# Three of four first mixings in three fp32r passes, POOL rounding and DVE subtracting, with a reordered first tile

## The chip, the cores and the metric

The kernel runs on one core of one Trainium2 chip. The metric is the device time of one execution in microseconds (us). Before the change it is 952.89 us, the median of three runs (951.13 to 954.56).

## The reference

Talking-heads attention, and behind it two feed-forward matmuls. Everything is fp32: q, k, v are 4 x 12 x 448 x 64, the two mixing matrices 12 x 12, `w_in` 768 x 2048 and `w_out` 2048 x 768. Cut to what matters:

```python
scores = np.matmul(q, k.transpose(0, 1, 3, 2)) / np.sqrt(64)
scores = np.einsum('bhij,hg->bgij', scores, w_pre)       # first mixing, over the heads
attn = np.exp(scores - scores.max(-1, keepdims=True))
attn = attn / (attn.sum(-1, keepdims=True) + 1e-09)
attn = np.einsum('bhij,hg->bgij', attn, w_post)          # second mixing
x = np.matmul(attn, v).transpose(0, 2, 1, 3).reshape(1792, 768)
h = x @ w_in
out = np.where(h >= 1, h, np.where(h <= -1, 0, (h + 1) ** 2 / 4)) @ w_out
```

The weights of the feed-forward part arrive as 64-bit floats and are turned into fp32 on the chip.

## The kernel before

**Tiles, blocks, groups.** The 448 query rows of each of the 4 batches are cut into tiles of 120, 120, 120 and 88 rows, 16 tiles in all. A tile is cut into blocks of up to 10 query rows with all 12 heads, so that a block fills 120 partitions (10 rows x 12 heads) with 448 keys. A tile of 120 rows has 12 blocks, one of 88 rows has 9; they are worked in three groups a tile, so there are 36 groups of four blocks and 12 of three, 48 groups and 180 blocks.

**One pass of the loop over groups** (`for n in range(NG + 2)`, L586) puts the work of several groups into each engine's queue in an order written out by hand. The scores of a tile lie in SBUF (`ssb`). `load_s` (L175) moves a block from there into the block layout by a DMA (queue SP). `pre` (L191) is the first mixing on TensorE (PE): `wpre` times the block. `row_max` (L202, VectorE, DVE) and `exps` (L207, ScalarE, ACT) make the softmax, `norm` (L213) the reciprocal sums on DVE and, on GpSimd (POOL), the second mixing's matrix scaled by them (`wr`, L221). `post` (L224) is the second mixing on PE and is run for the group before, behind `pre` of the present group. Then come the transposes and scores of later tiles, `pv` (the product with v) of earlier ones, and pieces of the conversion of `w_in` and of some of `w_out` (`convs`).

**The first mixing in two forms.** A block whose fp32 values go to PE as they are costs one fp32 matmul, which the trace shows as two records of L200. A block that `split` (L182) has cut into a high part (rounded to fp32r) and a low part (the difference) costs three fp32r matmuls (L198). `split` runs for group n + 1 while group n is worked, both of its operations on DVE: the cast at L187, the subtraction at L188. It takes the second and fourth block of a group (`[1::2]`; in a group of three the second alone), and group 0 has none: 82 blocks of 180. The four loads of a group are issued in the order 1, 3, 0, 2 (0, 2 for the missing ones in a group of three): first those that are split.

**The first tile.** The loads of q and k, ten matmuls of an identity matrix (`warm`, which computes nothing that is used), transposes of q and k with two warm matmuls ahead of each k pair but the first, scores of tile 0, loads of group 0, transposes of q of tile 1, 16 warm matmuls, and then the loop.

**The feed-forward part** goes in batches of 512, 512, 512 and 256 rows and 16 steps each; a step is `ffn1` (L419), `gate` (L431 to L436, ACT and DVE in turn, six dependent operations with the split), `ffn2` (L456) of the step before. In the first batch's steps the rest of `w_out` is converted: `lowest` (ACT, L288) writes a buffer `wk`, two of them, which the integer addition on POOL (L301) two steps later releases.

Of the kernel before, what the change touches and what calls it, by code (L numbers as in the profile page):

```python
# [9 lines left out]
F32 = mybir.dt.float32  # L10
F32R = mybir.dt.float32r
I32 = mybir.dt.int32
# [10 lines left out]
def tile_talking_heads_moe(  # L23
# [151 lines left out]
    def load_s(m):  # L175
        t, o, ni, c = blocks[m]
        n, nb = tiles[t][2:]
        x = ap_.tile([KM, S], F32, tag="s10", name="s10", bufs=8)
        nc.sync.dma_start(out=x[:ni * H], in_=ssb[t][o:n:nb])
        s10[m] = x  # L180

    def split(m):  # L182
        k = blocks[m][2] * H
        x = s10.pop(m)
        hi = ap_.tile([KM, S], F32R, tag="sh", name="sh", bufs=2)
        lo = ap_.tile([KM, S], F32R, tag="sl", name="sl", bufs=2)
        nc.vector.tensor_copy(out=hi[:k], in_=x[:k])  # L187
        nc.vector.tensor_tensor(out=lo[:k], in0=x[:k], in1=hi[:k].bitcast(F32), op=ALU.subtract)  # L188
        s10[m] = (hi, lo)

# [75 lines left out]
    def convert(st, p):  # L266

        def halves():
            w = st["raw"].bitcast(I32).rearrange("p (n t) -> p n t", t=2)
            return w[:, :, 0], w[:, :, 1]

        def scaled():
            lo, hi = halves()
            if "t" not in st:  # L280
                st["t"] = p.tile([128, CW], I32, tag="wt", name="wt", bufs=3)
            nc.scalar.activation(out=st["t"].bitcast(F32), in_=hi.bitcast(F32), func=AF.Copy,
                                 scale=2.0 ** -111)

        def lowest():
            lo, hi = halves()
            st["k"] = p.tile([128, CW], I32, tag="wk", name="wk", bufs=2)
            nc.scalar.activation(out=st["k"], in_=lo.bitcast(U32), func=AF.Copy, scale=2.0 ** -29)  # L288

        def shifted():  # L290
            nc.vector.tensor_single_scalar(out=st["t"], in_=st["t"], scalar=3,
                                           op=ALU.logical_shift_left)

        def sign():
            lo, hi = halves()
            t = st["t"]
            nc.vector.scalar_tensor_tensor(out=t, in0=hi, scalar=-0x80000000, in1=t,
                                           op0=ALU.bitwise_and, op1=ALU.bitwise_or)

        def add():  # L300
            nc.gpsimd.tensor_tensor(out=st["t"], in0=st["t"], in1=st.pop("k"), op=ALU.add)  # L301

        return [scaled, lowest, shifted, sign, add]
# [120 lines left out]
    def gate(s, ps):  # L424
        n = bat[steps[s][0]][1]
        a = pool['fw'].tile([128, TB], F32, tag="a", name="a")
        mx = pool['fw'].tile([128, TB], F32, tag="mx", name="mx")
        gh = pool['fw'].tile([128, TB], F32R, tag="gh", name="gh")
        gl = pool['fw'].tile([128, TB], F32R, tag="gl", name="gl")

        nc.scalar.activation(out=a[:, :n], in_=ps[:, :n], func=AF.Relu, scale=0.5, bias=c05)  # L431
        nc.vector.tensor_tensor(out=mx[:, :n], in0=ps[:, :n], in1=a[:, :n], op=ALU.max)  # L432
        nc.vector.scalar_tensor_tensor(out=mx[:, :n], in0=a[:, :n], scalar=1.0, in1=mx[:, :n],  # L433
                                       op0=ALU.min, op1=ALU.mult)
        nc.scalar.activation(out=gh[:, :n], in_=mx[:, :n], func=AF.Copy)  # L435
        nc.vector.tensor_tensor(out=gl[:, :n], in0=mx[:, :n], in1=gh[:, :n].bitcast(F32),  # L436
                                op=ALU.subtract)
        gs[s] = (gh, gl)
# [36 lines left out]
    with tc.manual_schedule():  # L475
# [22 lines left out]
                                base=H - 1, pattern=[[H, IB]], channel_multiplier=-1)  # L498

        def warm(n):  # L500
            ps = ps_q.tile([128, 128], F32, tag="q", name="ps_w")
            for m in range(n):
                nc.tensor.matmul(out=ps, lhsT=ident, rhs=ident, start=True, stop=True)

        warm(10)
        trans_q(0, 0)
        trans_k(0, 0)
        trans_q(0, 1)
        for hp in range(1, HP):
            warm(2)  # L510
            trans_k(0, hp)
        for g in range(3):
            scores(0, [2 * g, 2 * g + 1])()
# [16 lines left out]
        load_q(2)  # L530
        trans_q(1, 0)
        trans_q(1, 1)
        warm(16)
        at = {}
        late = {}

# [5 lines left out]
        for g in range(3):  # L542
            put(1, lambda g=g: load_v(0, g))
        for t in range(1, len(tiles)):
            for g in range(3):
                vis.setdefault(max(0, 3 * t - 4 + g), []).append((t, [2 * g, 2 * g + 1]))
            nb = tiles[t][0]
            if t >= 2:
                for g in range(2):
                    at.setdefault(3 * t - 6 + g, []).append(lambda t=t, g=g: trans_q(t, g))  # L550
                    if t + 1 < len(tiles):
                        put(3 * t - 6 + g, lambda t=t, g=g: load_q(t + 1, (g,)))
                if tiles[t][1] == 0:
                    for hp in range(HP):
                        put(3 * t - 7 + hp // 2, lambda nb=nb, hp=hp: load_k(nb, hp))
                        at.setdefault(3 * t - 6 + hp // 2, []).insert(0, lambda nb=nb, hp=hp: trans_k(nb, hp))
# [29 lines left out]
        for n in range(NG + 2):  # L586
            if n == NE:
                s_qk.close()
                pool['fp'] = ctx.enter_context(tc.tile_pool(name="ffn", bufs=2, side="right",
                                                            reuse_waits="tile"))  # L590
                pool['ps_h'] = ctx.enter_context(tc.tile_pool(
                    name="ps_h", bufs=2, space=PSUM, side="right", reuse_waits="tile"))
            if n == NG - 1:
                s_ss.close()
                pool['fw'] = ctx.enter_context(tc.tile_pool(name="ffw", bufs=2, side="right",
                                                            reuse_waits="tile"))
            share = nconv / (NE - 1)
            ms = groups[n] if n < NG else ()
            old = list(groups[n - 1]) if 0 < n <= NG else []
            if n + 1 < NG:  # L600
                for m in (*groups[n + 1][1::2], *groups[n + 1][::2]):
                    load_s(m)
            if ms:
                sm = ap_.tile([KM, 4], F32, tag="sm", name="sm", bufs=3)
            for m in ms:
                pre(m)
            nxt = list(groups[n + 1][1::2]) if n + 1 < NG else []
            for m in ms:
                row_max(m)
            if nxt:  # L610
                split(nxt.pop(0))
            for j, m in enumerate(ms):
                if j == 3:
                    post(old.pop(0)) if old else None
                exps(m, j, sm)
            if ms:
                norm(ms, sm)
            for m in nxt:
                split(m)
            convs(share * (n + 0.4))  # L620
            for m in old:
                post(m)
            for f in at.pop(n, ()):
                f()
            for t, g in vis2.pop(n, ()):
                pv(t, g)
            for f in [scores(t, hps) for t, hps in vis.pop(n, ())]:
                f()
            for f in late.pop(n, ()):
                f()  # L630
            convs(share * (n + 1))
            if n == NG:
                h = ffn1(0)
# [18 lines left out]
        for s in range(NS + 1):  # L652
            if s < NS:
                j, f = steps[s]
                if s > 0:
                    h = ffn1(s)
                    if f == NF - 1 and j + 1 < len(bat):
                        for kk in range(2, KDM):
                            split_x(j + 1, kk)
                            if kk == 2:  # L660
                                load_x(j + 1, KDM - 1)
                    gate(s, h)
                if j + 1 < len(bat):
                    if NF - 10 <= f < NF - 7:
                        load_x(j + 1, f - (NF - 10))
                    if NF - 6 <= f < NF - 4:
                        load_x(j + 1, f - (NF - 10) - 1)
            if s >= 1:
                ffn2(s - 1)
            if s + 2 < NS:  # L670
                split_w(s + 2)
            if s + NWE + 1 < NF:
                load_w(s + NWE + 1)
            for x in sorted(cv.pop(s, ()), key=lambda x: x[:3]):
                x[3]()
            if s < NS and j + 1 < len(bat):
                if NF - 8 <= f < NF - 6:
                    split_x(j + 1, f - (NF - 8))
# [29 lines left out]
```

## Time and profile before

| | |
|---|---|
| median of three runs | 952.89 us (951.13 to 954.56) |
| the profiled execution | 952.53 us |
| its span, first to last instruction | 950.6 us |
| PE busy | 932.6 us, 98% |
| DVE busy | 606.9 us, 64% |
| ACT busy | 543.0 us, 57% |
| POOL busy | 179.5 us, 19% |

The profiled execution is 1.93 us longer than its span, and 0.36 us below the median. Busy shares are means over the span: the attention part lasts until about 477 us and uses all engines and the DMA queues, the feed-forward part behind it uses PE nearly alone.

### The profile page before, as it was taken

Reading aid. Unit: us, or ns where it says so; the run is one execution under the profiler, and the core shown is the slowest. Engines: PE = TensorE matmul, PEld = TensorE weight load, DVE = VectorE, ACT = ScalarE, POOL = GpSimd, SP = SyncE. Lnnn points to the kernel's source line nnn. Section 1 sums busy time; section 2 is a strip of 40 time slices with the busy share of each in tenths; the row PEclk is TensorE's granted clock in tenths of the full one; section 3 lists DMA queues with packets and bytes.
Section 4 is the critical chain, followed back from the end, with each engine's and each line's share of the span. In section 5 each row is a group of like instructions: output and inputs, shape, how many; then the busy total and the mean of one; then the engine's idle time right before and its main releaser. Section 6 shows DMA issues by size and latency. Waiting matters only on the chain.

```text
span 950.6 us, 17979 instructions
## 1 busy us (share of the span) xinstructions
PE 932.6 (98%) x6754; PEld 785.2 (83%) x6754; DVE 606.9 (64%) x1113; ACT 543.0 (57%) x1146; POOL 179.5 (19%) x253
## 2 busy tenths in 40 slices
PE   7999999999999999999999989999999999999997
PEld 6677888888888888888888878888888888888997
DVE  3677867877778867765555566654455554445774
ACT  4576777776786767776655453533334433334553
POOL 0233234332434234331201212000000000000000
PEclk8999999999999999999999999999999999999999
DMA  5875766876677756745453440120000200000100
GB/s 90 223 220 165 202 188 205 244 208 180 202 214 229 209 159 205 235 159 147 140 205 140 157 164 1 38 74 1 12 12 12 83 1 1 12 1 20 54 1 34
DMA packets 118361, 115.21 MB, mean 121 GB/s; under 512 B 61700, under 2 KB 107268, under 8 KB 118276
## 3 DMA queue, kind: packets, MB, share of 16 engines
q1 hardware_dynamic: 115492, 113.38, 39.8%
q10 hardware_dynamic: 2784, 0.69, 0.5%
q8 instruction: 54, 0.88, 0.4%
q14 instruction: 31, 0.25, 0.1%
HBM read 55.85 MB, written 19.66 MB: 79 GB/s over the span
## 4 chain that ended last, share of the span: by engine, by line
PE 92%; DVE 2%; ACT 2%; DMA 1%; issue 1%; POOL 1%; SPq 0%; POOLq 0%; ACTq 0%
PE o L456 22%; PE ps_h L419 22%; PE ps_a L231 16%; PE ps_l L200 8%; PE ps_x L247 8%; PE ps_s L155 7%; PE ps_l L198 5%; PE ps_k L121 1%; DMA k<-in_k_dram 1%; PE ps_t L138 1%; POOL wo L301 1%; DMA s<-ssb 0%; DVE mx L433 0%; DVE wil L389 0%; DVE mx L432 0%
## 5 line engine op out<-in xcount | busy, mean ns | idle before, releaser
L221 POOL TENSOR_SCALAR wr<-wpost,rs 120x120 f32<-120x120 f32 x180 | 113.4, 647 | 306.7 <-DVE rs L217 273.2
L231 PEld LDWEIGHTS ps_a<-wr,e 120*112 120x112 f32 x1440 | 154.3, 177 | 6.7 <-issue 4.9
L231 PE MATMUL ps_a<-wr,e 120*112 120x120 f32 (+1 forms) x1440 | 155.2, 266 | 0.0
L210 ACT ACTIVATE e<-ps_l,nm 120x448 f32<-120x448 f32 x180 | 112.8, 632 | 56.8 <-DVE nm L204 56.2
L419 PE MATMUL ps_h<-xh,wil 128*128 128x512 f32 (+1 forms) x384 | 139.5, 363 | 0.0
L419 PE MATMUL ps_h<-xl,wih 128*128 128x512 f32 (+1 forms) x384 | 139.2, 362 | 0.0
L419 PE MATMUL ps_h<-xh,wih 128*128 128x512 f32 (+1 forms) x384 | 139.2, 362 | 0.0
L456 PE MATMUL o<-woh,gl 128*128 128x512 f32 x448 | 115.7, 339 | 4.4 <-DVE gl L436 4.4
L432 DVE TENSOR_TENSOR mx<-ps_h,a 128x512 f32<-128x512 f32 (+1 forms) x64 | 39.9, 624 | 119.3 <-ACT a L431 119.3
L456 PE MATMUL o<-woh,gh 128*128 128x512 f32 x448 | 115.5, 339 | 0.0
L456 PE MATMUL o<-wol,gh 128*128 128x512 f32 x448 | 115.3, 339 | 0.0
L204 DVE TENSOR_REDUCE nm<-ps_l 120x1 f32<-120x448 f32 x180 | 104.2, 618 | 14.7 <-PE ps_l L200 11.8
L431 ACT ACTIVATE a<-ps_h,c 128x512 f32<-128x512 f32 (+1 forms) x64 | 40.4, 632 | 112.7 <-PE ps_h L419 112.5
L233 ACT ACTIVATE aT<-ps_a 112x480 f32<-112x480 f32 x180 | 96.2, 591 | 3.0 <-PE ps_a L231 2.6
L200 PE MATMUL ps_l<-s,wpre 120*120 120x448 f32 x196 | 94.6, 567 | 1.6 <-ACT wk L288 1.6
L435 ACT ACTIVATE gh<-mx 128x512 fp32r<-128x512 f32 (+1 forms) x64 | 37.0, 578 | 92.8 <-DVE mx L433 92.8
L456 PEld LDWEIGHTS o<-woh,gl 128*128 128x128 f32 x448 | 75.1, 189 | 17.9 <-DVE gl L436 6.8
L456 PEld LDWEIGHTS o<-woh,gh 128*128 128x128 f32 x448 | 76.4, 188 | 9.8
L456 PEld LDWEIGHTS o<-wol,gh 128*128 128x128 f32 x448 | 76.3, 188 | 9.9
L247 PE MATMUL ps_x<-aT,v 112*64 112x120 f32 (+1 forms) x1536 | 83.8, 262 | 0.0
L419 PEld LDWEIGHTS ps_h<-xl,wih 128*128 128x128 f32 x384 | 72.4, 189 | 12.2
L419 PEld LDWEIGHTS ps_h<-xh,wih 128*128 128x128 f32 x384 | 72.4, 189 | 11.5
(75 smaller groups left out, 1462.7 us busy)
## 6 DMA issues: line engine op xcount, KB each, us to landing
s<-ssb SPq DMA_DIRECT2D x172, 210.0 KB
wraw<-in_moe_w_in_dram SPq DMA_DIRECT2D x32, 384.0 KB
raw<-in_moe_w_out_dram SPq DMA_DIRECT2D x20, 384.0 KB
wid<-wt SPq DMA_DIRECT2D x32, 192.0 KB
wi<-wid SPq DMA_DIRECT2D x16, 384.0 KB
v<-in_v_dram SPq DMA_DIRECT2D x12, 448.0 KB
out_dram<-osb SPq DMA_DIRECT2D x14, 384.0 KB
wraw<-in_moe_w_out_dram SPq DMA_DIRECT2D x12, 384.0 KB
```

The costliest lines, as they stand in the source:

```text
L155: nc.tensor.matmul(out=ps[s][:n], lhsT=qt[t][x][r, hp, :n], rhs=kt[b, hp][y][r, :], start=(m == 0), stop=(m == 2))
L198: nc.tensor.matmul(out=lps[m], lhsT=w[:k], rhs=y[:k], start=(j == 0), stop=(j == 2))
L200: nc.tensor.matmul(out=lps[m], lhsT=wpre[:k], rhs=x[:k], start=True, stop=True)
L204: nc.vector.tensor_reduce(out=nm, in_=lps[m], axis=AX.X, op=ALU.max, negate=True)
L210: nc.scalar.activation(out=e, in_=ps, func=AF.Exp, bias=nm, accum_out=sm[:, j:j + 1])
L221: nc.gpsimd.tensor_scalar_mul(out=w[:, :, :ni], in0=wpost[:, :, :ni], scalar1=rs[:, j:j + 1])
L231: nc.tensor.matmul(out=ps[:, r, :ni * H], lhsT=e[:, r * KP:(r + 1) * KP], rhs=w[:, :, :ni], start=True, stop=True)
L233: nc.scalar.activation(out=aT[t][:, :, :, c:c + ni], in_=ps[:, :, :ni * H].rearrange("q r (h i) -> q r h i", h=H), func=AF.Copy)
L247: nc.tensor.matmul(out=ps[s * D:(s + 1) * D, m, :n], lhsT=vt[b, g][:, 2 * m + s, r * D:(r + 1) * D], rhs=a[:, r, 4 * g + 2 * m + s, :n], s ...
L419: nc.tensor.matmul(out=ps[:, :n], lhsT=w[:, kk, :], rhs=x[:, :n], start=(c == 0), stop=(c == last))
L431: nc.scalar.activation(out=a[:, :n], in_=ps[:, :n], func=AF.Relu, scale=0.5, bias=c05)
L456: nc.tensor.matmul(out=o[bank][:, c0:c0 + ne], lhsT=g[:, t * 128:(t + 1) * 128], rhs=w[:, e0:e0 + ne], start=(f == 0 and m == 0 and c0 == ...
```

## The change

- `split` becomes two functions. The cast goes to POOL (`nc.gpsimd.tensor_copy`), the subtraction (`split_lo`) stays on DVE. Three blocks of four (two of three) are split: 129 blocks of 180. `sh` and `sl` get three buffers each instead of two, `s10`, the loaded blocks, six instead of eight.
- The loads of a group go in the order 1, 2, 3, 0.
- In the loop all casts of group n + 1 are queued on POOL ahead of the `wr` of group n.
- First tile: 12 warm matmuls at the start, three behind the first k pair, four and one ahead of the next two k pairs, none ahead of the others. The first third of tile 1's scores is computed ahead of the loop, where there were 16 warm matmuls; six stay.
- `wk` has six buffers in the feed-forward part.
- The last `ffn1` and its gate come one step earlier, ahead of `ffn2` of the third step from the end; its `gh` and `gl` get buffers of their own.

```diff
@@ load_s, split
-        x = ap_.tile([KM, S], F32, tag="s10", name="s10", bufs=8)
+        x = ap_.tile([KM, S], F32, tag="s10", name="s10", bufs=6)
...
-        hi = ap_.tile([KM, S], F32R, tag="sh", name="sh", bufs=2)
-        lo = ap_.tile([KM, S], F32R, tag="sl", name="sl", bufs=2)
-        nc.vector.tensor_copy(out=hi[:k], in_=x[:k])
+        hi = ap_.tile([KM, S], F32R, tag="sh", name="sh", bufs=3)
+        lo = ap_.tile([KM, S], F32R, tag="sl", name="sl", bufs=3)
+        nc.gpsimd.tensor_copy(out=hi[:k], in_=x[:k])
+        s10[m] = (x, hi, lo)
+
+    def split_lo(m):
+        k = blocks[m][2] * H
+        x, hi, lo = s10[m]
         nc.vector.tensor_tensor(out=lo[:k], in0=x[:k], in1=hi[:k].bitcast(F32), op=ALU.subtract)
         s10[m] = (hi, lo)
@@ lowest
-            st["k"] = p.tile([128, CW], I32, tag="wk", name="wk", bufs=2)
+            st["k"] = p.tile([128, CW], I32, tag="wk", name="wk", bufs=6 if p is pool.get("wp") else 2)
@@ gate
+        p, w, z = (pool['wp'], n, "z") if s == len(steps) - 1 else (pool['fw'], TB, "")
+        gh = p.tile([128, w], F32R, tag="gh" + z, name="gh" + z)
+        gl = p.tile([128, w], F32R, tag="gl" + z, name="gl" + z)
@@ the first tile
-        warm(10)
+        warm(12)
         trans_q(0, 0)
         trans_k(0, 0)
+        warm(3)
         trans_q(0, 1)
         for hp in range(1, HP):
-            warm(2)
+            warm((4, 1, 0, 0, 0)[hp - 1])
             trans_k(0, hp)
...
-        warm(16)
+        scores(1, [0, 1])()
+        warm(6)
...
-            for g in range(3):
+            for g in range(t == 1, 3):
                 vis.setdefault(max(0, 3 * t - 4 + g), []).append((t, [2 * g, 2 * g + 1]))
@@ the loop over groups
-                for m in (*groups[n + 1][1::2], *groups[n + 1][::2]):
+                for m in (*groups[n + 1][1:], groups[n + 1][0]):
                     load_s(m)
...
-            nxt = list(groups[n + 1][1::2]) if n + 1 < NG else []
+            nxt = list(groups[n + 1][1:]) if n + 1 < NG else []
             for m in ms:
                 row_max(m)
+            for m in nxt:
+                split(m)
             if nxt:
-                split(nxt.pop(0))
+                split_lo(nxt.pop(0))
...
                 norm(ms, sm)
             for m in nxt:
-                split(m)
+                split_lo(m)
@@ the feed-forward steps
-                if s > 0:
+                if 0 < s < NS - 1:
                     h = ffn1(s)
...
                     gate(s, h)
+
+                    if s == NS - 2:
+                        gate(NS - 1, ffn1(NS - 1))
```

The first place is PE's queue at the program's start, the difference of the two kernels. `ps_w` are the warm matmuls, `ps_t` the transposes of q, `ps_k` those of k.

```order
-L503 MATMUL ps_w<-ident 128x128 x10
+L512 MATMUL ps_w<-ident 128x128 x12
 L138 MATMUL ps_t<-ident,qraw 128x120 x3
 L121 MATMUL ps_k<-ident,k_86 128x112 x4
+L512 MATMUL ps_w<-ident 128x128 x3
 L138 MATMUL ps_t<-ident,qraw 128x120 x3
-L503 MATMUL ps_w<-ident 128x128 x2
+L512 MATMUL ps_w<-ident 128x128 x4
 L121 MATMUL ps_k<-ident,k_86 128x112 x4
-L503 MATMUL ps_w<-ident 128x128 x2
```

More warm matmuls stand ahead of the second k pair; the pairs behind the third follow each other with none between, where two stood ahead of each.

The second place is DVE's queue in the loop pass of group 2, in the kernel before. `nm` is the row maximum, `s_556` and `s_558` are two loaded blocks of group 3, `rs` the reciprocal sums, `wt` a weight chunk under conversion.

```order
L204 TENSOR_REDUCE nm<-ps_l 120x1 x4
L187 CAST sh<-s_556 120x448
L188 TENSOR_TENSOR sl<-s_556,sh 120x448
L216 TENSOR_SCALAR rs<-sm 120x4
L217 RECIPROCAL rs<-rs 120x4
L187 CAST sh<-s_558 120x448
L188 TENSOR_TENSOR sl<-s_558,sh 120x448
L291 TENSOR_SCALAR wt<-wt 128x384
L297 SCALAR_TENSOR_TENSOR wt<-wraw,wt 128x384
```

The same place in the changed kernel, where the three blocks of group 3 are `s_554`, `s_556` and `s_558`:

```order
L209 TENSOR_REDUCE nm<-ps_l 120x1 x4
L193 TENSOR_TENSOR sl<-s_554,sh 120x448
L221 TENSOR_SCALAR rs<-sm 120x4
L222 RECIPROCAL rs<-rs 120x4
L193 TENSOR_TENSOR sl<-s_556,sh 120x448
L193 TENSOR_TENSOR sl<-s_558,sh 120x448
L296 TENSOR_SCALAR wt<-wt 128x384
L302 SCALAR_TENSOR_TENSOR wt<-wraw,wt 128x384
```

The casts are gone from DVE and a third subtraction has come, behind the reciprocal sums like the second.

The third place is POOL's queue in the same stretch of the changed kernel, from the `wr` of group 1 to the casts for group 4. Before, POOL had only the rows of `wr` (four a group) and `wt` (the integer addition of a weight chunk) here, in this order.

```order
L226 TENSOR_SCALAR wr<-wpost,rs 120x120 x4
L306 TENSOR_TENSOR wt<-wt,wk 128x384
L187 CAST sh<-s_554 120x448
L187 CAST sh<-s_556 120x448
L187 CAST sh<-s_558 120x448
L226 TENSOR_SCALAR wr<-wpost,rs 120x120 x4
L306 TENSOR_TENSOR wt<-wt,wk 128x384
L187 CAST sh<-s_671 120x448
```

The three casts for group 3 now stand ahead of the `wr` of group 2 and of the addition behind it, and wait for group 3's loads.

## Rows read from the trace of the kernel before

**Rows 1.** The page: span, and busy time of each engine.

```profile
span 950.6 us, 17979 instructions
PE 932.6 (98%) x6754; PEld 785.2 (83%) x6754; DVE 606.9 (64%) x1113; ACT 543.0 (57%) x1146; POOL 179.5 (19%) x253
```

**Rows 2.** Busy time in stretches: length, engines, TensorE's granted clock, DMA share, GB/s.

```profile
35.00:40.00 5.00, 4.84 (x18) 3.02 (x19) 2.72 (x6) 2.63 (x6) 0.71 (x2) 0.66 0.92 242
40.00:50.00 10.00, 10.00 (x73) 8.27 (x72) 8.77 (x18) 8.59 (x22) 3.74 (x5) 1.00 0.97 209
...
200.00:300.00 100.00, 100.00 (x940) 82.38 (x939) 77.75 (x165) 73.53 (x183) 37.41 (x53) 1.00 0.69 203
```

**Rows 3.** Waits of PE: us in total, times, longest.

```profile
PE o L456 <- DVE gl L436: 4.4, 6, 1.2
PE ps_l L200 <- ACT wk L288: 1.6, 1, 1.6
```

**Rows 4.** The chain that ended last, 20 to 60 us: start, us, what.

```profile
55.34 0.98 PE ps_l L200 x2
56.33 0.61 PE ps_l L198 x3
56.94 0.75 PE ps_l L200 x2
```

**Rows 5.** Timeline of the first tile's end: start, us, engine, line, count.

```profile
21.56 1.24 DVE L164 COPY ssb<-ps_s 120x448 f32<-120x448 f32 x2 [0.35 <-PE ps_s L155]
...
22.88 3.28 SPq L179 DMA_DIRECT2D s<-ssb  x4
...
24.13 3.84 PE L503 MATMUL ps_w<-ident 128*128 128x128 f32 x32 [1.23 <-DVE ql L141]
...
27.80 3.17 PE L200 MATMUL ps_l<-s,wpre 120*120 120x448 f32 x8
```

**Rows 6.** Groups of instructions by line: the split on DVE.

```profile
L188 DVE TENSOR_TENSOR sl<-s,sh 120x448 fp32r<-120x448 f32 (+1 forms) x82 | 54.2, 661 | 2.8
...
L187 DVE CAST sh<-s 120x448 fp32r<-120x448 f32 (+1 forms) x82 | 31.0, 378 | 36.5 <-DMA s<-ssb 36.5
```

**Rows 7.** Groups of instructions on POOL, shapes apart.

```profile
L221 POOL TENSOR_SCALAR wr<-wpost,rs 120x120 f32<-120x120 f32 x172 | 107.8, 643 | 306.7 <-DVE rs L217 273.2 <-PE ps_a L231 19.5 <-PE ps_x L247 7.6
L301 POOL TENSOR_TENSOR wt<-wt,wk 128x384 int32<-128x384 int32 x44 | 44.2, 1007 | 0.0
...
masks.py:199 POOL TENSOR_SCALAR_AFFINE_SELECT ident<-ident 128x128 f32<-128x128 f32 x1 | 0.3, 294 | 0.1
...
L497 POOL TENSOR_SCALAR_AFFINE_SELECT mask<-mask 120x10 f32<-120x10 f32 x1 | 0.2, 196 | 0.1
```

**Rows 8.** Timelines of DVE and PE where a group's loads are late.

```profile
52.62 0.39 DVE L187 CAST sh<-s 120x448 fp32r<-120x448 f32 x1 [2.89 <-DMA s<-ssb]
...
171.28 0.39 DVE L187 CAST sh<-s 120x448 fp32r<-120x448 f32 x1 [1.95 <-DMA s<-ssb]
...
174.89 1.01 PE L200 MATMUL ps_l<-s,wpre 120*120 120x448 f32 x2
...
450.21 0.39 DVE L187 CAST sh<-s 120x448 fp32r<-120x448 f32 x1 [3.01 <-DMA s<-ssb]
...
451.62 0.98 PE L200 MATMUL ps_l<-s,wpre 120*120 120x448 f32 x2
```

**Rows 9.** Timeline, 196 to 216 us: POOL's `wr` and the `post` that reads it.

```profile
199.81 2.41 POOL L221 TENSOR_SCALAR wr<-wpost,rs 120x120 f32<-120x120 f32 x4 [5.33 <-DVE rs L217]
...
207.21 3.44 PE L231 MATMUL ps_a<-wr,e 120*112 120x120 f32 x32
```

**Rows 10.** Timeline of ACT in a feed-forward step.

```profile
563.20 0.55 ACT L288 ACTIVATE wk<-raw 128x384 int32<-128x384 uint32 x1 [2.61 <-POOL wo L301]
```

**Rows 11.** Timeline of the last steps: DVE's last `wil`, PE's last `ffn2`.

```profile
935.33 0.96 DVE L389 SCALAR_TENSOR_TENSOR wil<-wi,wih 128x768 fp32r<-128x768 f32 x1 [0.31 <-ACT wih L388]
...
943.64 0.61 PE L456 MATMUL o<-woh,gl 128*128 128x512 f32 x2 [0.40 <-DVE gl L436]
```

More of the change, by code (lines that the diff above doesn't have):

```diff
@@ L427, in gate @@
         mx = pool['fw'].tile([128, TB], F32, tag="mx", name="mx")
-        gh = pool['fw'].tile([128, TB], F32R, tag="gh", name="gh")
-        gl = pool['fw'].tile([128, TB], F32R, tag="gl", name="gl")
+        p, w, z = (pool['wp'], n, "z") if s == len(steps) - 1 else (pool['fw'], TB, "")
+        gh = p.tile([128, w], F32R, tag="gh" + z, name="gh" + z)
+        gl = p.tile([128, w], F32R, tag="gl" + z, name="gl" + z)
         nc.scalar.activation(out=a[:, :n], in_=ps[:, :n], func=AF.Relu, scale=0.5, bias=c05)
@@ L500, in warm @@
         def warm(n):
+            if n == 0:
+                return
             ps = ps_q.tile([128, 128], F32, tag="q", name="ps_w")
```

## The prediction

> **What bounds the kernel now.** The page comes first: PE is busy 932.6 of 950.6 us [rows 1]. Busy is no proof of a bound, so the stretches come next: from 200 to 300 us PE has no idle time at all, DVE is at 78%, ACT at 74%, POOL at 37% and the DMA engines at 0.69 [rows 2]. PE sets the pace of the attention part, with DVE as the nearest follower. PE's own waits say where it stands still later: 4.4 us for `gl` in the feed-forward part and 1.6 us once near 55 us [rows 3]. The rest of the loss lies ahead of 28 us and in one place behind: from 35 to 40 us the granted clock is 0.66 [rows 2], that is, PE ran about 3.4 of those 5 us at its lower level of 1.2 GHz. So the change can win in three ways: less PE work in the attention part, those 4.4 us, and the first tile.
>
> **First mixing, PE.** In the chain a split block takes 0.61 us (three passes), an unsplit one 0.75 us; the first block of a group, 0.98 us, stays unsplit [rows 4]. Of the 35 groups of four behind group 0, and of the 12 groups of three, each gets one more split block: 47 blocks, 0.14 us each. PE is the bound there, so this is taken in full, but for the three blocks of groups 1 to 3, which lie ahead of a load that PE waits for anyway (below): 44 x 0.14 = **6.2 us**. Bounds: 0, if the split arrives late, and 47 x 0.14 = 6.6.
>
> **The split, DVE.** 82 casts of 378 ns go (31.0 us) and 47 subtractions of 661 ns come (31.1 us) [rows 6]. DVE's total is unchanged, and as it had 22% idle [rows 2] I cost it at nothing. If that cover were gone, each further 0.1 us a group would cost 4.7 us in all.
>
> **The split, POOL.** 129 casts of 120x448 come; the trace has no such operation on POOL. Two simple selections without a second input took 196 ns for 10 elements a partition and 294 ns for 128 [rows 7], a slope of 0.83 ns, so 0.56 us for 448: the lower bound. The two-input integer addition took 1.007 us for 384 elements, which gives 1.17 us; `wr` took 643 ns for 120, which by its rate would be 2.4 us, the upper bound [rows 7]. The cast is one-input and streams like the selections; I take **0.7 us**. A group of four then asks 2.1 us for casts, 2.4 for `wr` [rows 9] and 1.0 for the addition, 5.5 us. The period is 9.2 us: `pre` of groups 16 and 46 start at 174.89 and 451.62 [rows 8], 30 groups apart. POOL has room.
>
> The casts stand ahead of `wr`, so what `wr` loses counts. Four `wr` began at 199.81 and the first is read at 207.21 [rows 9]: 7.4 us of slack for a delay of 2.1 us, or 3.5 at 1.17. No cost. DVE now waits for POOL ahead of its first subtraction, which delays the reciprocal sums by 0.7 - 0.38 = 0.3 us where the load is late: covered by the same slack. The third subtraction has most to lose. In the late group of 171.28 us the first load landed then; the last split block is wanted at 174.89 + 0.98 + 2 x 0.61 = 177.1 [rows 4, 8], 5.8 us on. Three casts and one subtraction in a row are 2.8 us (4.2 at 1.17). Hidden.
>
> The Trainium skill (GPSIMD Engine Reference, section 4.1) sends elementwise work to VectorE, and its key points say that POOL shares its SBUF interfaces with VectorE and contends with instructions of two SBUF inputs, which the subtraction is. No row here shows a POOL cast; by that rule, an estimate, every cast could stand behind a subtraction, 0.7 + 0.66 us, and a group would ask 7.5 us of POOL. That is still under the period, so the sum would be the same, and only the rival below comes nearer.
>
> **The loads' order.** Block 0, first in `pre`, now comes fourth instead of third (third instead of second in a group of three). SP issues the four loads in 3.28 us, 0.82 apart [rows 5]; as they land I put them 0.8 to 1.4 us apart. From 171.28 the fourth lands at 173.7 to 175.5, and PE wants it at 174.89 less 0.14: a toss-up, in the few groups that are this late. I take 0.3 us for all, 0 to 4 as bounds. In group 46 the first of three loads came at 450.21, after a wait of 3.01 us, and `pre` began at 451.62 [rows 8]: the second load had landed by then, the third by 453.0 at 1.4 apart. I take **-1.3 us** (0 to -1.6). Six buffers instead of eight cost nothing: the load that is fourth in the next group needs the buffer of a block whose subtraction lies a whole group back.
>
> **The first tile.** Tile 0's last scores leave DVE at 22.80 us, the first loads are issued at 22.88, and `pre` starts only at 27.80, behind 16 warm matmuls of 3.84 us [rows 5]. 32 records in 3.84 us are 0.24 us a matmul at full clock. Between the second k pair and the scores seven fewer stand: 1.7 us at full clock, 3.4 at half. Copies of k on ACT and DVE follow in their own time, so I let the loads start **1.5 us** earlier (1 to 2.2). Then the DMA queues take over: their share is 0.92 from 35 to 40 us and 0.97 from 40 to 50 [rows 2]. So the scores moved ahead and the shorter warm-up do not shorten the way to group 3, whose first load arrives at 52.62 after a wait of 2.89 us [rows 8], and for which PE waits 1.6 us [rows 3]. There I keep the 1.5 us, less 0.8 for the fourth load. PE idles longer in front of group 3 than before; if the clock falls there, half of some 3.4 us [rows 2], 1.7 us, goes. First tile: **+0.7 us**, bounds -1.0 and +3.3 (1.5 + 1.8 if the queues have room).
>
> **`wk`.** In each step of the first batch ACT stood 2.61 us at `lowest` until POOL's addition released a buffer [rows 10], and everything of ACT behind it, the gate among them, came late; five of PE's six waits for `gl` are these, 4.4 less the last of 0.40: **4.0 us** [rows 3, 11]. Six buffers hold two chunks for three steps, so the wait goes. What is late next: without this wait neither ACT nor DVE has a step's worth of work, so PE becomes the bound of these steps as it is of the later ones. Bounds 3 and 4.
>
> **The last step.** PE's last wait, 0.40 us [rows 11], goes, because the last gate now runs under two `ffn2`. The earlier `ffn1` needs `wil`, which DVE finished at 936.29 [rows 11], just as the `ffn1` before it ends. **0.4 us**, bounds 0 and 0.5.
>
> **Sum.** 6.2 - 0.3 - 1.3 + 0.7 + 4.0 + 0.4 = 9.7 us. From the profiled execution, 952.53 us, this gives **942.8 us**. That execution lies 0.36 us under the median of its kernel's runs; I add nothing for it.
>
> **Rivals.** A change of 0.3%, 2.9 us, is about what a measurement of this kernel can tell from none.
>
> *Late loads eat the first mixing's gain.* Idle time of DVE's casts was all for loads, 36.5 us [rows 6]. Against it speaks that PE itself hardly waited. If a third of the 47 groups lose 0.4 us, 6.4 us go: 949.
>
> *The split becomes the pace at no net gain.* If casts and subtractions exclude each other and a cast takes 1.17 us, the chain of three is 3 x (1.17 + 0.66) = 5.5 us against the 5.8 us from above; with 0.3 us lost in most groups, 0.3 x 35 = 10.5 us, all that was won goes: 952.
>
> *Slower: POOL becomes the bound.* At 2.2 to 2.4 us a cast a group of four asks 3 x 2.2 + 2.4 + 1.0 = 10.0 us of POOL against 9.2: 35 x 0.8 = 28 us lost, the 6.2 not won, 3.5 from the other parts: 977. It decides from a cast of about 2.0 us on, or 1.4 where it also stands out every subtraction. For it speaks only the rate of `wr`, which at 120 elements is mostly a fixed cost.
>
> *The DMA queues give way.* First tile +3.3, no late loads: 938.6.
>
> **How the numbers follow.** The forecast, 938.5 to 947: 0.68. Late loads, 947 to 950: 0.10. More gain than 938.5: 0.07. No net gain, 950 to 955.4: 0.07. POOL bound: 0.08. Faster by over 0.3% (under 950.0): 0.85; within: 0.07; slower: 0.08. The range, 937.5 to 949, leaves out the last two cases and the edges, 2 in 10; the ends of the terms together make 938 to 949.
>
> **What would show it.** Right: L193 129 times near 0.66 us on DVE, POOL's casts at 0.6 to 0.9 us, PE without waits between 60 and 440 us, `gl` gone from PE's waits, pairs of 0.61 in the chain. A wait of PE for a load at group 46, near 1.3 us, shows the price of the order. Wrong: PE waiting for `sl`, `wr` late behind casts, POOL above 80% busy in the attention part, or the clock at 1.2 GHz for a second stretch around 50 us.

## The result, and the profile after

The changed kernel took 958.43 us (median of 8 runs, 955.56 to 964.15); the kernel before took 953.21 us beside it (8 runs, 951.13 to 955.51). The ratio is 1.0061, 95% interval 1.0037 to 1.0085: slower by 0.6%, where 942.8 us had been forecast. The profiled execution took 957.07 us.

The page after, with the lines that answer to [rows 1]: PE is busy for 6.1 us less than before, and yet the span is 4.3 us longer.

```profile
span 954.9 us, 18250 instructions
...
PE 926.5 (97%) x6781; PEld 795.1 (83%) x6781; DVE 612.9 (64%) x1078; ACT 539.8 (57%) x1146; POOL 286.3 (30%) x382
```

PE's waits after, the longest entry (in us: total, times, longest). Against [rows 3] the wait for `gl` is gone from the list, and a wait of the unsplit block for its load has come.

```profile
PE ps_l L205 <- DMA s<-ssb: 15.8, 8, 3.1
```

Windows after: the stretch that had no idle time in [rows 2], and three in which the granted clock (the third number from the end) falls; 0.50 is 1.2 GHz.

```profile
52.00:58.00 6.00, 4.42 (x14) 3.58 (x15) 5.32 (x12) 1.40 (x5) 5.42 (x9) 0.72 0.55 201
...
150.30:153.70 3.40, 3.22 (x12) 2.88 (x12) 3.31 (x8) 1.72 (x5) 3.05 (x6) 0.50 0.82 236
...
266.30:269.70 3.40, 3.40 (x13) 3.07 (x14) 3.40 (x7) 1.96 (x6) 2.65 (x5) 0.50 0.79 264
...
200.00:300.00 100.00, 96.22 (x910) 82.59 (x910) 74.97 (x151) 69.82 (x177) 57.09 (x76) 0.98 0.66 195
```

Groups of instructions on POOL and DVE after, for [rows 6, 7]. The cast takes 643 ns where 0.7 us was assumed, and the subtraction what it took before; but POOL's casts now stand idle for 147.1 us waiting for loads, and DVE's subtractions for 68.3 us waiting for the casts.

```profile
L226 POOL TENSOR_SCALAR wr<-wpost,rs 120x120 f32<-120x120 f32 x180 | 136.5, 772 | 20.2 <-DVE rs L222 17.8 <-PE ps_a L236 2.1 <-DMA s<-ssb 0.3
L187 POOL CAST sh<-s 120x448 fp32r<-120x448 f32 x129 | 82.7, 643 | 190.2 <-DMA s<-ssb 147.1 <-PE ps_a L236 30.5 <-PE ps_l L203 5.7
...
L193 DVE TENSOR_TENSOR sl<-s,sh 120x448 fp32r<-120x448 f32 x129 | 81.5, 643 | 68.4 <-POOL sh L187 68.3
```

Where the time went is read from the start of `pre` in PE's timelines, group by group. "No split" is the second experiment below, which has everything of the change but the split.

| start of `pre`, us | before | after | no split | store late | mixed |
|---|---|---|---|---|---|
| group 4 | 63.1 | 62.8 | 62.1 | 62.9 | 61.4 |
| group 12 | 138.6 | 137.0 | 137.5 | 137.5 | 136.0 |
| group 14 | 156.7 | 159.7 | 155.8 | 155.3 | 153.8 |
| group 24 | 250.4 | 253.6 | 249.4 | 248.8 | 247.1 |
| group 26 | 268.4 | 275.5 | 267.5 | 266.6 | 264.9 |
| group 36 | 362.1 | 368.8 | 361.2 | 361.9 | 358.4 |
| group 38 | 380.2 | 388.9 | 379.4 | 379.7 | 376.2 |
| group 45 | 444.2 | 452.1 | 443.4 | 444.3 | 440.4 |
| group 47 | 458.2 | 468.7 | 457.9 | 458.7 | 455.4 |
| first `ffn1` | 469.1 | 479.5 | 468.9 | 469.4 | 466.2 |
| end of the span | 950.6 | 954.9 | 944.3 | 945.3 | 941.6 |

From group 4 to 12 the changed kernel gains as forecast: 74.2 us against 75.5. Then it loses in jumps: 4.6 us from group 12 to 14, 3.9 from 24 to 26, 2.0 from 36 to 38, 2.6 from 45 to 47 (each the difference of the two stretches). Between the jumps it wins little or nothing: 93.9 us against 93.7 from group 14 to 24. The first three jumps lie right behind groups of three blocks (9 to 11, 21 to 23, 33 to 35), the last within such. The feed-forward part gives back 6.1 us (481.5 to 475.4, from the first `ffn1` to the end).

The first jump in detail. SP's queue around the loads of group 13, before and after (the loads of group 12 are the first of four, those of group 13 the second); SP only issues the DMAs here, in this order, and waits at the head of its queue.

```profile
131.47 3.38 SPq L179 DMA_DIRECT2D s<-ssb  x4
...
138.94 0.34 SPq L330 DMA_DIRECT2D wod<-wt  x1
139.37 0.39 SPq L323 DMA_DIRECT2D wraw<-in_moe_w_in_dram  x1
139.85 3.38 SPq L179 DMA_DIRECT2D s<-ssb  x4
```

```profile
129.31 0.34 SPq L335 DMA_DIRECT2D wid<-wt  x1
130.02 3.35 SPq L179 DMA_DIRECT2D s<-ssb  x4
133.42 0.50 SPq L328 DMA_DIRECT2D wraw<-in_moe_w_in_dram  x1
139.36 0.34 SPq L335 DMA_DIRECT2D wod<-wt  x1
139.80 1.28 SPq L328 DMA_DIRECT2D wraw<-in_moe_w_in_dram  x1
141.13 3.42 SPq L179 DMA_DIRECT2D s<-ssb  x4
```

POOL in the same stretch (the bracket is the idle time ahead of an instruction and what ended it).

```profile
132.97 0.56 POOL L187 CAST sh<-s 120x448 fp32r<-120x448 f32 x1 [3.69 <-DMA s<-ssb]
133.87 0.75 POOL L187 CAST sh<-s 120x448 fp32r<-120x448 f32 x1 [0.33 <-DMA s<-ssb]
134.76 1.03 POOL L187 CAST sh<-s 120x448 fp32r<-120x448 f32 x1
135.78 2.57 POOL L226 TENSOR_SCALAR wr<-wpost,rs 120x120 f32<-120x120 f32 x3
138.32 1.97 POOL L306 TENSOR_TENSOR wt<-wt,wk 128x384 int32<-128x384 int32 x2
```

And PE, at the `pre` of group 13:

```profile
148.72 0.98 PE L205 MATMUL ps_l<-s,wpre 120*120 120x448 f32 x2 [2.97 <-DMA s<-ssb]
```

Read in order of time: the loads of group 12 are issued from 130.02 on. The casts take them as they land; the third starts at 134.76. `wr` and then the conversion's additions stand behind the casts, so the first addition ends at about 139.3 (half of 1.97 us behind 138.32). The store on SP waits for it (139.36), the load of weights stands behind the store, and the loads of group 13 behind both, at 141.13. PE waits 2.97 us for the last of them. From 150.3 the granted clock is 0.50 for 3.4 us, which costs half of that, 1.7 us; 2.97 and 1.7 make the jump of 4.6.

That is a loop: the loads of one group depend, through split, addition and store, on the landings of the group before. A turn is the time from issue to issue. The loop was there before the change too, through the splits on DVE, and PE did not wait: the turn from 131.47 to 139.85 took 8.4 us, in a pass of 8.0 (`pre` of groups 11 and 12 start at 130.6 and 138.6). Now it takes 11.1 us, from 130.02 to 141.13, in a pass of 7.8 (129.2 to 137.0). Of the 2.7 us more, 1.9 lie between the issue and the store and 0.9 at the load of weights, which held SP for 1.28 us instead of 0.39; why it did so is not shown. This pass is a short one, the last of three blocks, and the group that is loaded in it has four blocks and three splits. The turns at groups 25 and 37, in passes of 7.8 us as well, take 10.4 and 10.1 us, where they took 8.4 each. SP's waits for the addition, at the store, before and then after (us in total, times, longest):

```profile
SPq L330 <- POOL wt L301: 53.3, 15, 5.4
```

```profile
SPq L335 <- POOL wt L306: 66.4, 20, 6.1
```

The wait as such costs nothing, as the first line shows; it costs where a turn outlasts the pass.

The jump at the end, in groups 45 to 47, is another case: no store stands ahead of the loads of group 46. The loads on SP, the two casts on POOL and `pre` on PE, after:

```profile
450.87 2.57 SPq L179 DMA_DIRECT2D s<-ssb  x3
```

```profile
460.05 0.56 POOL L187 CAST sh<-s 120x448 fp32r<-120x448 f32 x1 [7.43 <-DMA s<-ssb]
461.31 0.56 POOL L187 CAST sh<-s 120x448 fp32r<-120x448 f32 x1 [0.70 <-DMA s<-ssb]
```

```profile
462.33 0.98 PE L205 MATMUL ps_l<-s,wpre 120*120 120x448 f32 x2 [2.88 <-DMA s<-ssb]
```

The first of the three lands 9.2 us after the issue (before 8.3, from 441.94 to 450.21), the issue comes 1.3 us ahead of its pass instead of 2.2, and block 0, which PE wants first, lands third instead of second, 1.0 us behind the second. Added up (0.9, 0.9 and 1.0) they come to PE's 2.9 us; no run changed them one by one.

### The profile page after: what moved, and what is told of

Same layout as the page of the kernel before. It is cut to its first block, busy times and chain, and to the rows that moved or that the text cites. A ratio compares the mean times of both kernels' runs of the same rounds, so it can differ in the third digit from the quotient of the medians.

```text
span 954.9 us, 18250 instructions
## 1 busy us (share of the span) xinstructions
PE 926.5 (97%) x6781; PEld 795.1 (83%) x6781; DVE 612.9 (64%) x1078; ACT 539.8 (57%) x1146; POOL 286.3 (30%) x382
## 4 chain that ended last, share of the span: by engine, by line
PE 87%; DMA 6%; DVE 2%; POOL 1%; ACT 1%; issue 1%; SPq 0%; POOLq 0%; ACTq 0%; DVEq 0%
PE o L463 25%; PE ps_h L424 24%; PE ps_a L236 13%; PE ps_l L203 7%; PE ps_x L252 7%; PE ps_s L155 6%; DMA s<-ssb 5%; PE ps_l L205 4%; PE ps_k L121 1%; PE ps_t L138 1%; POOL wr L226 1%; POOL sh L187 1%; DMA qraw<-in_q_dram 1%; DVE wt L302 1%; DVE ssb L164 1%
## 5 line engine op out<-in xcount | busy, mean ns | idle before, releaser
L236 PE MATMUL ps_a<-wr,e 120*112 120x120 f32 (+1 forms) x1440 | 157.3, 267 | 1.4 <-ACT e L215 1.4
L226 POOL TENSOR_SCALAR wr<-wpost,rs 120x120 f32<-120x120 f32 x180 | 136.5, 772 | 20.2 <-DVE rs L222 17.8
L187 POOL CAST sh<-s 120x448 fp32r<-120x448 f32 x129 | 82.7, 643 | 190.2 <-DMA s<-ssb 147.1
L193 DVE TENSOR_TENSOR sl<-s,sh 120x448 fp32r<-120x448 f32 x129 | 81.5, 643 | 68.4 <-POOL sh L187 68.3
L463 PE MATMUL o<-woh,gh 128*128 128x512 f32 (+1 forms) x444 | 114.6, 339 | 0.0
L463 PE MATMUL o<-wol,gh 128*128 128x512 f32 (+1 forms) x444 | 114.1, 339 | 0.0
L463 PE MATMUL o<-woh,gl 128*128 128x512 f32 (+1 forms) x444 | 114.0, 338 | 0.0
L209 DVE TENSOR_REDUCE nm<-ps_l 120x1 f32<-120x448 f32 x180 | 102.0, 618 | 7.7 <-PE ps_l L205 5.8
L463 PEld LDWEIGHTS o<-wol,gh 128*128 128x128 f32 x444 | 75.5, 188 | 9.9
```

The source lines that it names most:

```text
L187: nc.gpsimd.tensor_copy(out=hi[:k], in_=x[:k])
L209: nc.vector.tensor_reduce(out=nm, in_=lps[m], axis=AX.X, op=ALU.max, negate=True)
L226: nc.gpsimd.tensor_scalar_mul(out=w[:, :, :ni], in0=wpost[:, :, :ni], scalar1=rs[:, j:j + 1])
L236: nc.tensor.matmul(out=ps[:, r, :ni * H], lhsT=e[:, r * KP:(r + 1) * KP], rhs=w[:, :, :ni], start=True, stop=True)
L463: nc.tensor.matmul(out=o[bank][:, c0:c0 + ne], lhsT=g[:, t * 128:(t + 1) * 128], rhs=w[:, e0:e0 + ne], start=(f == 0 and m == 0 and c0 == ...
```

## The experiments

The theory behind the trace: **the loop** (loads wait on SP behind a store that waits for the splits). Rivals: the **order** of the loads alone; **six buffers** hold the loads; **POOL**, its casts or its contention with DVE; the **first tile**. All times stand beside runs of the kernel before on the same chip, 951.7 to 952.3 us.

**1. The two feed-forward edits alone, and 2. all but the split.** The first is the kernel before with `wk` and the last step as in the diff above; the second has the new first tile too.

> The kernel before with the two edits of the feed-forward part alone (six buffers wk, the last ffn1 early). My sum gave 4.0 + 0.4 us for them. If the loss sits in the attention part alone, as the starts of pre in the two traces say, this kernel is 4 to 6 us faster than before, ratio 0.994 to 0.996, and PE has no wait for gl. If these edits cost something as well, it comes out within 2 us of before.

> The changed kernel with the split, the loads' order and the buffers of before (so before with the new first tile and the two edits of the feed-forward part). If the split and what it does to the queues is the loss, this kernel keeps 4 us from the feed-forward part and 0.5 to 3 us from the first tile: 945 to 949 us, ratio near 0.994. If the new first tile is the loss (group 3 comes late and the clock falls at 55 us), it is no better than before with the feed-forward edits alone, 949 us or more, and PE still has waits for loads in groups 13, 25, 37 and 46.

Measured: 946.09 us, ratio 0.9934 (0.9909 to 0.9959), and 946.06 us, 0.9925 (0.9903 to 0.9947). So the feed-forward edits bring 6.0 us and the first tile nothing: in both traces the first `ffn1` starts at 468.9. The split then loses 10.6 us, by the spans of number 2 (944.3) and of the change (954.9); by the medians, each against its runs of the kernel before, it is 11.3. With the new first tile PE is 6.1 us ahead of the kernel before at group 2 (39.9 against 46.1) and 1.1 at group 4; between them it waits for the loads of group 3:

```profile
PE ps_l L200 <- DMA s<-ssb: 5.3, 3, 4.4
```

**3. The unsplit block loaded third.**

```diff
-                for m in (*groups[n + 1][1:], groups[n + 1][0]):
+                for m in (*groups[n + 1][1:-1], groups[n + 1][0], groups[n + 1][-1]):
```

> The changed kernel with the unsplit block loaded third of four, as before (in a group of three second of three). If the loads' order is the loss, PE's 26.9 us of waits for loads shrink to a few and the time falls by 8 us or more, to 950 or less. If all loads of these groups come late together because SP issues them late (my theory after the trace: the conversion's addition stands behind the casts on POOL, the store and the load of weights behind the addition on SP), the order gives back 0.8 us in each of some five late groups, 1 to 4 us in all: 953 to 957.

Measured: 973.91 us, ratio 1.0231 (1.0202 to 1.0260), a result that none had expected. The waits for loads did shrink, from 15.8 to 2.8 us, but others took their place; PE's longest waits are now for what stands behind the last cast on POOL and ACT:

```profile
PE ps_l L203 <- POOL wr L226: 8.5, 5, 2.2
PE ps_a L236 <- ACT e L215: 6.1, 6, 1.2
PE ps_l L205 <- DMA s<-ssb: 2.8, 2, 1.6
```

The third split block now lands fourth, everything behind it comes a landing later, and SP's waits for the addition rise from 66.4 to 81.4 us. So the order matters, the other way round: not for the block that PE wants first, but for the split that lands last.

**4. The casts on DVE.** `nc.vector.tensor_copy` in place of `nc.gpsimd.tensor_copy`, in the same place of the order.

> The changed kernel with all 129 casts on DVE in place of POOL, in the same place of the program's order, so ahead of the subtractions. DVE gets 129 x 0.378 = 49 us more work. If casts on POOL hold up the conversion's addition and with it SP's queue, the waits for loads go and the time falls under 950, though DVE, then at some 85 to 88% in the attention part, may pace some groups. If the third split block or the loads themselves are the loss, it stays at 955 or more.

Measured: 965.36 us, ratio 1.0132 (1.0105 to 1.0159). PE waits 16.5 us for loads, 3.7 us of it at group 13, 1.9 at 25 and 2.0 at 37. So the loss needs no cast on POOL: DVE now waits for the landings with everything behind it, `wr` and the addition behind DVE, and SP waits 76.0 us for the addition. But DVE also has 49 us more work here, so this run alone does not clear POOL; number 8 does.

**5. The store a chunk later.** This cuts the loop at the store: the store no longer needs the addition that has only just been queued.

```diff
-        lags = ((store, 8), (4, 6), (2, 4), (3, 4), (1, 3), (0, 2), (load, 0))
+        lags = ((store, 11), (4, 6), (2, 4), (3, 4), (1, 3), (0, 2), (load, 0))
...
-                st["t"] = p.tile([128, CW], I32, tag="wt", name="wt", bufs=3)
+                st["t"] = p.tile([128, CW], I32, tag="wt", name="wt", bufs=3 if p is pool.get("wp") else 4)
```

> The changed kernel with the conversion's store issued one weight chunk later (three slots) and a fourth buffer wt in the attention part. New theory, after the runs so far: a loop. The loads of group n+1 stand on SP behind a store, the store waits for POOL's addition, the addition stands behind the splits of group n, and these wait for the loads of group n; three split blocks make it wait for the third of four landings and three casts. Where a turn of the loop (issue to issue, 11.1 us at group 12 to 13) is longer than PE's pass, PE waits. With the store a chunk later the loop is cut: waits of PE for loads go at groups 13, 25, 37 and 46, the clock stays up, and the time is that of the kernel without the split less 44 x 0.14 us, 939 to 942. If the loads themselves are slow or six buffers hold them, it stays above 953.

Measured: 948.65 us, ratio 0.9971 (0.9957 to 0.9984): better than the change by 0.9% (the two ratios) or 9.6 us (the spans, 945.3 against 954.9), though not the 939 to 942 expected. The jumps at groups 13, 25 and 37 are gone (table), and 0.6 us is left of PE's wait at group 46. SP's waits for the addition, and its queue in the stretch shown above:

```profile
SPq L335 <- POOL wt L306: 1.2, 2, 0.8
```

```profile
130.48 3.38 SPq L179 DMA_DIRECT2D s<-ssb  x4
133.92 0.50 SPq L335 DMA_DIRECT2D wid<-wt  x1
134.47 0.43 SPq L328 DMA_DIRECT2D wraw<-in_moe_w_in_dram  x1
135.01 3.42 SPq L179 DMA_DIRECT2D s<-ssb  x4
```

The loads of group 13 are issued at 135.01 instead of 141.13, 6.1 us earlier, with the casts where they were (the first at 133.40 instead of 132.97). The fourth buffer `wt` does not explain it: in the changed kernel ACT stood ahead of its writes of `wt` for loads of weights alone, 4.1 us, and never for a store. What is still lost lies in groups 17, 19, 29, 31, 32 and 41, and at 19 it is another queue. DVE, then PE:

```profile
198.49 0.62 DVE L193 TENSOR_TENSOR sl<-s,sh 120x448 fp32r<-120x448 f32 x1 [2.18 <-POOL sh L187]
...
200.75 0.63 DVE L193 TENSOR_TENSOR sl<-s,sh 120x448 fp32r<-120x448 f32 x1 [0.46 <-POOL sh L187]
...
202.90 0.62 DVE L128 TENSOR_TENSOR kl<-ps_k,kh 128x448 fp32r<-128x448 f32 x1
```

```profile
203.62 0.98 PE L205 MATMUL ps_l<-s,wpre 120*120 120x448 f32 x2 [0.74 <-PE ps_s L155]
```

The first subtraction waits 2.18 us and the last ends at 201.4; behind it in this pass stand the conversion and the casts and subtractions of k. The loads of group 19 had all landed by 200.7. Its first mixing takes the PSUM buffer that the first transposed k pair leaves (the sixth one back), and `kl` of that pair ends at 203.52, just ahead of 203.62. (The releaser that the row names, the scores on PE, had long been done.)

**6. The splits behind `wr` and half of the conversion.** The three casts and the three subtractions move behind `convs(share * (n + 0.4))`.

> The changed kernel with the three casts and three subtractions queued behind the matrices wr and behind the first half of the pass's conversion. By the loop theory additions of the first half no longer stand behind the casts, only those of the second half do, so the loop is loosened: 940 to 950. If splits are simply late for PE (the chain of casts and subtractions sets the pace), putting them later costs more: 960 or above.

Measured: 1070.81 us, ratio 1.1250 (1.1232 to 1.1269). The rival's line came true, for this order: PE now waits for DVE in nearly every pass (26 times for `sl` alone). There is no room to put the splits late.

```profile
PE ps_l L203 <- DVE xo L263: 12.3, 7, 2.3
PE ps_l L203 <- DVE kl L128: 11.0, 8, 2.4
...
PE ps_l L203 <- DVE ql L141: 10.7, 9, 2.2
...
PE ps_l L203 <- DVE sl L193: 9.0, 26, 0.5
```

**7. Six buffers alone.** The kernel of experiment 1 with `bufs=6` for `s10`.

> The kernel before with the two edits of the feed-forward part and six buffers of loaded blocks in place of eight, nothing else. By the loop theory, and by my prediction's 'six buffers cost nothing', it equals the kernel with eight, 946 us. If six buffers hold the loads, it loses most of the 10 us that the split lost: 950 to 957.

Measured: 947.30 us, ratio 0.9951 (0.9934 to 0.9968). Beside 0.9934 with eight the intervals overlap; the buffers are not the 10 us. In the profiled executions six buffers cost 2.6 us of span (947.0 against 944.4), all of it at group 3, where PE waits 2.5 us for a load (0.6 with eight); a microsecond or two can't be ruled out.

**8. Two splits on POOL, landing first and second; 9. the same two, landing first and third.** Number 8 is the changed kernel with `[1::2]` and the loads' order of before, 9 differs from 8 in the order of the loads alone: 1, 0, 3, 2 in place of 1, 3, 0, 2 (in groups of three 0, 1, 2 in place of 1, 0, 2).

> The changed kernel with two of four blocks split (one of three) and the loads of the split blocks first, as before; the casts stay on POOL, and six buffers. By the loop theory the splits wait for the second landing and for two casts, as before, so nothing is lost: 944 to 947, like the kernel without the changed split. If POOL's casts or six buffers are the loss, it stays at 950 or more.

> The kernel with two split blocks of four on POOL (946.2 us with the split blocks loaded first and second) with another order of the loads alone: the second split block is now loaded third (in a group of three the one split block second), as the last one is in the changed kernel. The loop theory, sharpened: what counts is on which landing a pass's last split waits, since everything behind it on POOL and DVE waits with it. It then loses a good part of the 10 us again, 950 to 957. If the number of split blocks (POOL's and DVE's work) is the loss, it stays at 945 to 948.

Measured: 946.17 us, ratio 0.9940 (0.9924 to 0.9956), and 957.61 us (951.24 to 960.70), 1.0042 (1.0021 to 1.0062). With POOL's casts and six buffers, but two splits and early landings, nothing is lost; one exchange in the loads' order brings a loss of 1.0%, some 10 us, with the same work. The profiled execution of 9 was its fastest, 951.24 us, and shows half of that: its span is 949.5 us, 5.1 more than that of 8. PE waits 0.9, 1.3 and 0.8 us at groups 13, 25 and 37, the groups of the jumps, and 1.5 at 46. None of these waits is for a load: the first three are put down to DVE's `ql`, those at 46 to a cast and a `wr` on POOL. In this execution the late landing thus reaches PE through DVE's and POOL's queues, not through a load. Where the slower executions of 9 lose the rest is not shown.

The four orders together: last split block landing second, 946.2; third, 957.6 with two splits and 958.4 with three; fourth, 973.9.

**10 and 11. Loads issued earlier.** The loads of group n + 2 stand at the end of pass n, ahead of its loads of q, k and v and its second half of the conversion; 11 has the late store too.

> The changed kernel with the loads of group n+2 issued at the end of pass n, ahead of that pass's loads of q, k and v and of the second half of its conversion, instead of the loads of group n+1 at the start of the pass. This takes one store, one load of weights and the loads of k out of the way of the loads, so the loop is shorter by 1 to 4 us a turn. By the loop theory most of the waits behind group 3 go: 939 to 948. If the landings are late because of the DMA queues and not because of the issue, it stays at 953 or more.

> The same with the store a chunk later as well (the edit that gave 948.7 us). What was left there were waits of 0.5 to 1 us in groups 17, 19, 29, 31, 32 and 41, where the subtractions wait for landings and DVE's copies of scores and k stand behind them. With loads a quarter of a pass earlier these go too: 937 to 942. If DVE's work itself is the limit in these passes, they stay and the time is 945 to 949.

Measured: 998.49 us, ratio 1.0488 (1.0460 to 1.0516), and 1001.76 us, 1.0517 (1.0490 to 1.0545). Both theories were wrong on this edit, since it brings a wait of its own. SP's waits in number 10:

```profile
SPq L179 <- DVE ssb L164: 157.9, 26, 12.6
SPq L179 <- DVE sl L193: 22.9, 21, 3.7
```

At the head of SP's queue the loads wait for score copies and buffers that are not ready so early, 157.9 us for the copies against 47.7 in the changed kernel, and the loads of k behind them come late: PE waits 10.2 us for these. The runs say nothing for or against the loop.

**12. Mixed.** The late store, and in the 15 groups 1 to 3, 17 to 21, 29 to 33, 41 and 46 only two splits (one in a group of three), in the old loads' order.

> The store a chunk later, and only two blocks split (loaded first and second) in the 15 groups 1 to 3, 17 to 21, 29 to 33, 41 and 46, where that kernel still lost time; three in the 32 others. If those losses come from the third split alone, the 32 groups keep 0.14 us each: 946 less 4.5, 940 to 943. If the later store costs something of its own, 944 or more.

Measured: 943.66 us, ratio 0.9903 (0.9885 to 0.9921), the fastest kernel here, 9 us under the kernel before. The page, and PE's longest wait, 3.8 us of which is the one at group 3:

```profile
span 941.6 us, 18182 instructions
...
PE 925.1 (98%) x6766; PEld 788.3 (84%) x6766; DVE 604.2 (64%) x1063; ACT 538.7 (57%) x1146; POOL 270.5 (29%) x367
...
PE ps_l L205 <- DMA s<-ssb: 5.1, 4, 3.8
```

The 32 groups bring 2.4 us against number 2 (946.06) where 4.5 were expected; at the first `ffn1` the trace shows 2.7. Part of the rest is still lost in single groups (1.0 us at group 41, where `post` waits for ACT).

## Why the prediction was wrong

**Right.** A split block costs 0.14 us less: from group 4 to 12 eight further split blocks gained 1.25 us by the starts of `pre`, 0.16 each. POOL's cast took 0.64 us (0.7 assumed), DVE's total hardly moved (606.9 to 612.9), POOL at 30% was no bound. Nor did each cast wait for a whole subtraction, as the estimate of 0.7 + 0.66 us had it. `wr` went from 643 to 772 ns; experiment 5, faster than the change, has it at 783, so this is not the loss. A rule of the Trainium skill (Perfetto Trace Analysis, Optimizing Scalar/DVE Operations) says that work moved between DVE and POOL might not help, because they share a read port of SBUF: the longer `wr` agrees with sharing, the time of experiment 5 does not make it a reason here.

**The step that failed** is "The casts stand ahead of `wr`, so what `wr` loses counts ... No cost". It named one thing queued behind the casts and gave its slack, 7.4 us. It did not go on along POOL's queue to the conversion's addition, from there to the store at the head of SP's queue, and from there to the next group's loads: on that path a turn went from 8.4 to 11.1 us in a pass of 7.8, and PE waited 3.0, 2.0 and 1.3 us for loads at groups 13, 25 and 37. Experiment 5 cuts the loop at the store alone and takes 9.6 us of span back; 8 excludes POOL, its casts and the six buffers as such.

**The second step** is "The loads' order". It priced one block that lands fourth when PE wants it, 0.3 us in all; the price lies in the split that lands last (experiments 8 and 9, some 10 us for an exchange of two loads). At group 46 the term was right in kind and too small, -1.3 us: PE waited 2.9, of which the order is the 1.0 us from the second landing to the third; the later issue and the longer way to the landing were not in it.

**The clock** was looked for only in the first tile, where the sign of being wrong came true: the granted clock is 0.72 from 52 to 58 us, which is 3.4 us at 1.2 GHz, beside a wait of 3.1 us for the loads of group 3. The waits of 2.97 and 2.0 us ahead of groups 13 and 25 were each followed by 3.4 us at a granted clock of 0.50, from 150.3 and 266.3 us on: 1.7 us each. Those of 1.3 us at group 37 and 2.9 us at group 46 were followed by no such stretch.

**The rival** "Late loads eat the first mixing's gain" had the symptom and not the size: it took lost time in many groups and 0.4 us in each. It was few groups and 2 to 5 us in each. For a slower kernel there was POOL as the bound alone; POOL was busy for 57 to 60% from 100 to 400 us.

**Sums.** The lower ends of the terms, 0 - 4 - 1.6 - 1.0 + 3 + 0, make a loss of 3.6 us and 956 us, not the 949 at which the range ends; the profiled execution, 957.07, lies just above even that. A cast that stands out every subtraction makes POOL the bound from 1.3 us on (1.93 less 0.66), not 1.4.

**Sizes.** `wk` and the last step were to bring 4.4 us and brought 6.0. The starts of `ffn1` show it: between the starts of steps 8 and 13 (counted from 0) of the first batch, 535.4 and 582.3 us, the kernel before loses 5.4 us to experiment 1, where its five waits for `gl` add up to 4.0 [rows 3, 11]. The first tile, +0.7, brought nothing. That six buffers cost nothing is not shown (2.6 us of span in experiment 7).

**Open.** Experiment 5 is 1.0 us of span behind number 2, where the split was to bring 6.2, so some 7 us are still lost. How much of that is DVE's queue was read from one pass (group 19) and from number 12, which avoids it; no run changed that queue alone. How the executions of number 9 differ is open as well.

## What to carry to other kernels

When an operation that waits for a DMA is put ahead in an in-order queue, list everything behind it on that engine and follow it through the other queues until it ends or comes back to the same DMA. If it comes back, compare one turn, from issue to issue, with the shortest pass, not with the mean one. Between such operations the number counts less than on which landing the last of them waits; a store that lets the addition get a pass ahead is the cheap place to cut.

## What the hardware showed that was not expected

A wait of PE cost more than its row: the five waits for `gl` show 0.5 to 1.2 us, 4.0 in all, and cost 5.4 by the starts of `ffn1`, each some 0.28 us more than its row, the short ones as the long ones. The profile's ends of matmuls are modelled, so a part of such a gap may be counted as busy; no run separates this. And of a wait's cost on PE over a third can lie behind it: at group 13 it was 2.97 us of idle time and 1.7 us of the 3.4 us that followed at 1.2 GHz.

`wr` on POOL became longer without a cast beside it. In experiment 4, with all casts on DVE, it takes 771 ns, in the changed kernel 772; in experiment 8, with POOL's casts but 82 subtractions, 682, and in the kernel before, with 82 as well, 647. So it goes more with the 129 subtractions on DVE than with the casts on POOL.

```profile
L226 POOL TENSOR_SCALAR wr<-wpost,rs 120x120 f32<-120x120 f32 x180 | 136.4, 771 | 309.5 <-DVE rs L222 253.7 <-PE ps_s L155 24.2 <-PE ps_k L121 10.2
```
